# Output stores on another DMA queue, transposes one step earlier, and an exp ahead of an evacuation, in an attention + feed-forward kernel

## The chip, the cores and the metric

The kernel runs on one core of one Trainium2 chip. The metric is the device time of one execution in microseconds (us). Eight runs of the kernel before lie between 308.92 and 311.36 us, with a median of 310.46 us. A core has five engines with instruction queues of their own[...]: TensorE (PE: matrix multiplication into PSUM), VectorE (DVE), ScalarE (ACT), GpSimd (POOL) and SyncE (SP). In this kernel two of the queues issue DMAs: SP, whose transfers appear in the profile as the hardware queue q1, and POOL, whose transfers appear as the software queue q0. Both use the same 16 DMA engines.

## The reference

Attention for 8 batches of 8 heads, 576 tokens and head width 64. In front of each batch's keys and values stand 16 "beacon" keys and values that every query may see. The result is laid out as 4608 rows of 512 and goes through a feed-forward part:

```python
k_all = concatenate([beacon_k, k]);  v_all = concatenate([beacon_v, v])
a = softmax(q @ k_all.T / 8, causal on the 576 keys, free on the 16 beacons)
x = (a @ v_all) as 4608 x 512
h = (x @ w1) * (x @ w2) @ w3
out = h @ w_out            # 4608 x 512, float32
```

The last two products are linear, so the kernel forms `Wt = w3 @ w_out` once and then needs only `out = ((x @ w1) * (x @ w2)) @ Wt`. Matrix operands are fp16, sums and output are fp32.

## The kernel before

**Attention.** The work of a batch is cut into 8 steps `s`: four pairs of heads, two halves each (`NSB` = 8 steps a batch, `r = s % 8` is the place in the batch, `b = s // 8` the batch). A step needs `scores(s)` (line 446, two groups j = 0 and 1 of 4 to 10 matmuls, each into one of the two PSUM buffers `ps`), `exps(s, j)` (line 461, ACT: exp of `ps` into the SBUF tile `pT`), `mask(s, j)` (line 473, DVE: causal mask on the diagonal blocks; group 1 has none) and `values(s)` (6 or 24 matmuls with `va` on line 489, in even and odd steps, then the division by the row sums on DVE, lines 506 and 507, into `x16`).

**Feed-forward.** It is a Python generator, `stream()`, with one matmul of 512 columns to a unit. The 4608 rows are 9 chunks `mc` of 512. A chunk is 64 units of line 366 (`ff_ab`: for each of 8 column blocks a chain of four matmuls with w1, which ACT evacuates to `a_sb` on line 378, and a chain of four with w2, which DVE multiplies by `a_sb` into `gT` on line 380), and 32 units of line 400 (`ff_out`: four chains of eight matmuls with `Wt`; DVE evacuates each to `ot` on line 410, and line 411 stores the 128 x 512 fp32 tile, 256 KB, in HBM). `ot` has 8 buffers. All accumulations share three PSUM buffers `pm`. The evacuation is emitted with the last matmul of its chain.

**Order of the work.** The schedule is manual: each engine executes its instructions in the order in which the Python code emits them. The first 16 steps (batches 0 and 1) and the preparation of the weights follow the written list `ORDER`. Then 48 units are emitted, step 16's scores and exps, 8 more units and step 16's masks; and then the loop over steps 16 to 63 (lines 668 to 691), which mixes a number of units, `fill[s]`, into each step: 8 in steps 16 to 26, 12 or 13 in later ones. What is left when the steps are done (212 units) runs alone. One pass of the loop emits the scores and the first exp of step s + 1, `values(s)`, the first k1 of the units, the second exp and first mask of s + 1, and then the rest of the units. At 8 units a step, a step holds one whole column block: a chain with w1 and a chain with w2.

**Data of the batches.** `va`, `q16`, `k16`, `qT` and `kT` have two buffers, used by batches in turn. POOL issues the loads (lines 127, 136 and 140), which cast fp32 to fp16 on the way. At the end of the first pass of batch b (r = 0) it gets the `va` loads of batch b + 1, which must wait until step 8b - 1 has used the buffer, and behind them those of q and k of batch b + 2. SP issues the DMA transposes: `transpose_qk` (lines 151 and 152) makes `qT` and `kT` of batch b + 1 out of `q16` and `k16`, one of five chunks of tokens a pass, in passes r = 1 to 5; line 518 turns a finished batch's `x16` into columns of `xT` (two transposes in pass r = 6, three in pass r = 7), which the feed-forward part reads. SP also issues the stores of line 411. Each queue issues in the order in which the code emits, and each DMA queue has 8 semaphores in turn, so that a DMA also waits for the eighth one before it on its queue to land.

Of the kernel before, what the change touches and what calls it, by code (L numbers as in the profile page):

```python
# [12 lines left out]
ds, ts = bass.ds, bass.ts  # L13
# [50 lines left out]
def kernel(  # L64
# [13 lines left out]
    nc = tc.nc  # L78
    B, H, S, D = q.shape
    Nb = beacon_k.shape[2]  # L80
    P = 128
# [3 lines left out]
    M = B * S  # L85
    NKT = DM // P
    NFT = DF // P
    NJT = 5
# [36 lines left out]
    def load_q(b, c):  # L125
        rows = min(P, S - c * P)
        nc.gpsimd.dma_start(  # L127
            q16s[b % NB2][:rows, c, :].rearrange("s (h d) -> s h d", h=H),
            q[b, :, ds(c * P, rows), :].rearrange("h s d -> s h d"),
        )  # L130
# [11 lines left out]
    def load_k(b, jt):  # L142
        load_kv(b, jt, k, beacon_k, k16s[b % NB2][:, jt, :].rearrange("s (h d) -> s h d", h=H))

    def load_v(b, jt):
        load_kv(b, jt, v, beacon_v, vas[b % NB2][:, jt, :, 0:64])

    def transpose_qk(b, c):
        i = b % NB2
        rows = min(P, S - c * P)  # L150
        nc.sync.dma_start_transpose(qTs[i][:, :, ds(c * P, rows)], q16s[i][:rows, c, :])  # L151
        nc.sync.dma_start_transpose(kTs[i][:, :, ds(c * P, P)], k16s[i][:, c, :])  # L152
# [135 lines left out]
    for what, st in zip(FIRSTS[:7], homes):  # L288
# [7 lines left out]
        fill=0.0,  # L296
# [3 lines left out]
    for m, base in (  # L300
# [10 lines left out]
            fill=0.0,  # L311
# [84 lines left out]
    def ff_out(mc, gT):  # L396
        for mt in range(4):
            pm = psM.tile([P, 512], FP32, name="pm")
            for kf in range(NFT):
                nc.tensor.matmul(  # L400
                    pm,
                    gT[:, kf, ts(mt, P)],
                    Wt[:, kf, :],
                    start=(kf == 0),
                    stop=(kf == NFT - 1),
                )
                if kf < NFT - 1:
                    yield
            ot = op.tile([P, DM], FP32, name="ot")
            nc.vector.tensor_scalar(ot, pm, float(1.0 / GS), None, ALU.mult)  # L410
            nc.sync.dma_start(out[ds(mc * 512 + mt * P, P), :], ot)
            yield

    def stream():

        gT = yield from ff_ab(0, range(len(made), NFT), g0)
        yield from ff_out(0, gT)
        for mc in range(1, M // 512):
            gT = yield from ff_ab(mc)
            yield from ff_out(mc, gT)  # L420
# [6 lines left out]
    def emit_ff(n):  # L427
        nonlocal emitted
        for _ in range(n):
            try:  # L430
                next(ff)
            except StopIteration:
                return
            emitted += 1
# [17 lines left out]
    def scores(s):  # L452
        for j in range(2):
            score(s, j)

    def exps(s, j):
        g = 2 * (s % 2) + j
        if s // 2 not in pTs:
            pTs[s // 2] = ptp.tile([P, 2, PW], FP16, name="pT")
        pT = pTs[s // 2]  # L460
        nc.scalar.activation(  # L461
            pT[:, :, ds(GO[g], GW[g])], pss[s, j][:, :, 0 : GW[g]], AF.Exp, scale=scale
        )

    def mask(s, j):
        g = 2 * (s % 2) + j
        pT = pTs[s // 2]
        if g == 1:
            return
        m = {0: MA, 2: MB, 3: MB[:, 0:80]}[g]  # L470
        n = m.shape[1]
        blk = pT[:, :, ds(GO[g], n)]
        nc.vector.tensor_tensor(  # L473
            blk, blk, m.unsqueeze(1).to_broadcast([P, 2, n]), ALU.mult
        )
# [46 lines left out]
    def values(s):  # L522
        value_sums(s)
        normalize(s)

    NSB = 2 * NT
    NS = B * NSB
    fill = [0] * NS
# [7 lines left out]
    def ahead(s):  # L536
        scores(s)
        for j in range(2):
            exps(s, j)

    def masks(s):
        for j in range(2):
            mask(s, j)
# [119 lines left out]
        emit(*word.split("."))  # L663
    emit_ff(48)
    ahead(2 * NSB)
    emit_ff(8)
    masks(2 * NSB)
    for s in range(2 * NSB, NS):
        b, r = s // NSB, s % NSB
        more = s + 1 < NS  # L670
        if more:
            scores(s + 1)
            exps(s + 1, 0)
        values(s)
        k1 = min(4, fill[s])
        emit_ff(k1)
        if more:
            exps(s + 1, 1)
            mask(s + 1, 0)
        emit_ff(fill[s] - k1)  # L680
        if more:
            mask(s + 1, 1)
        if b < B - 1:
            if r == 0:
                for c in range(NJT):
                    load_v(b + 1, c)
                for c in range(NJT if b + 2 < B else 0):
                    load_q(b + 2, c)
                    load_k(b + 2, c)
            if 1 <= r <= NJT:  # L690
                transpose_qk(b + 1, r - 1)
    emit_ff(1 << 30)
# [1 line left out]
_INS = ['q', 'k', 'v', 'beacon_k', 'beacon_v', 'moe_w1', 'moe_w2', 'moe_w3', 'moe_w_out']  # L694
# [26 lines left out]
```

## Time and profile before

| what | value |
|---|---|
| median of 8 runs | 310.46 us |
| the profiled execution's own time | 310.35 us |
| its span, first to last instruction | 308.5 us |
| PE busy | 291.5 us (94% of the span) |
| DVE, ACT and POOL busy | 167.8, 157.9 and 114.6 us |
| granted PE clock, mean | 0.994 |
| DMA queues q0 and q1, share of 16 engines' span | 84.5% and 39.9% |
| HBM read and written | 39.32 and 9.44 MB |

The profile has one execution. Of a group of instructions it gives the busy time, the mean of one in ns, and the idle time of the engine ahead of them with what ended it. A timeline row gives start, duration, engine, line, operation, shape, the count, and in brackets the idle time before the first with what ended it; neighbours of one form are merged, so a row can be longer than the work in it. A matmul's end is modelled, so intervals from start to start are the safer measure.

### The profile page before, as it was taken

What the parts mean: (1) busy time and instruction counts of PE and PEld (TensorE: products, weight loads), DVE (VectorE), ACT (ScalarE), POOL (GpSimd) and SP (SyncE); (2) the same over time, 40 slices, a digit from 0 to 9 for tenths busy, and PEclk for the clock granted to TensorE, in tenths of its full rate; (3) what the DMA queues carried; (4) which work ended last, traced back from release to release, by engine and by line L of the source; (5) the groups of instructions that cost most, each with busy time, mean ns of one, the idle gap of its engine ahead of it and who ended that gap; (6) DMA issues with size and microseconds to landing.
All of it is one profiled execution on the core that took longest, in us unless ns stands there. A gap on an engine that the chain in (4) does not pass through costs nothing.

```text
span 308.5 us, 6956 instructions
## 1 busy us (share of the span) xinstructions
PE 291.5 (94%) x2804; PEld 148.4 (48%) x2804; DVE 167.8 (54%) x388; ACT 157.9 (51%) x224; POOL 114.6 (37%) x155
## 2 busy tenths in 40 slices
PE   7789989999889999979999999999999999999995
PEld 2345556554344455435555555455555554444442
DVE  5566757873455565535555555556555554343442
ACT  2448949921565666634566466546654660330320
POOL 4489498755645595049304930410000000000000
PEclk9999999999999999979999999999999999999999
DMA  7999999999999999999996999996333003302003
GB/s 277 307 159 183 186 151 168 141 138 145 230 141 155 156 142 212 149 162 162 170 199 77 160 195 156 114 193 125 72 75 141 0 12 70 135 0 102 34 2 136
DMA packets 162048, 42.67 MB, mean 138 GB/s; under 512 B 152288, under 2 KB 155872, under 8 KB 162016
## 3 DMA queue, kind: packets, MB, share of 16 engines
q0 software_dynamic: 109792, 17.57, 84.5%
q1 hardware_dynamic: 52224, 24.66, 39.9%
q8 instruction: 22, 0.36, 0.5%
q14 instruction: 10, 0.08, 0.1%
HBM read 39.32 MB, written 9.44 MB: 158 GB/s over the span
## 4 chain that ended last, share of the span: by engine, by line
PE 70%; DMA 13%; ACT 6%; POOL 3%; SPq 3%; DVE 2%; issue 2%; DVEq 0%; ACTq 0%
PE pm L366 32%; PE pm L400 18%; PE pv L489 9%; PE ps L446 7%; DMA qT<-q 5%; ACT pT L461 4%; DMA k<-in_k_dram 3%; DMA pT<-in_moe_w_dram 3%; PE pm L356 2%; DMA xT<-in_moe_w_dram 2%; ACT a_sb L378 2%; SPq L152 1%; POOL va L136 1%; DVE gT L380 1%; SPq L151 1%
## 5 line engine op out<-in xcount | busy, mean ns | idle before, releaser
L366 PE MATMUL pm<-xT,w 128*128 128x512 f16 x576 | 134.3, 382 | 0.5 <-ACT xT L232 0.5
L461 ACT ACTIVATE pT<-ps 128x768 f16<-128x768 f32 (+3 forms) x128 | 104.7, 864 | 41.9 <-PE ps L446 40.4
L366 PEld LDWEIGHTS <-w 128*128 128x128 f16 x576 | 53.6, 98 | 59.8 <-issue 3.3
L378 ACT ACTIVATE a_sb<-pm 128x512 f32<-128x512 f32 x69 | 41.2, 597 | 78.9 <-PE pm L366 78.3
L380 DVE TENSOR_TENSOR gT<-pm,a_sb 128x512 f16<-128x512 f32 x72 | 49.8, 691 | 49.8 <-PE pm L366 47.6
L400 PE MATMUL pm<-Wt,gT 128*128 128x512 f16 x288 | 65.8, 379 | 0.0
L136 POOL DMA_DIRECT2D va<-in_v_dram x40 | 33.8, 857 | 53.0 <-PE pv L489 46.8
L446 PE MATMUL ps<-qT,kT 64*128 64x80 f16 (+3 forms) x704 | 37.7, 228 | 5.3 <-ACT pT L461 2.9
L489 PE MATMUL pv<-va,pT 128*128 128x65 f16 x960 | 41.2, 194 | 1.5 <-DVE pT L473 1.5
L400 PEld LDWEIGHTS <-gT 128*128 128x128 f16 x288 | 27.2, 98 | 30.6
L489 PEld LDWEIGHTS <-pT 128*128 128x128 f16 x960 | 33.4, 98 | 12.0 <-issue 5.1
L506 DVE RECIPROCAL rd<-pv 128x4 f32<-128x4 f32 x64 | 12.1, 189 | 47.6 <-PE pv L489 47.2
L446 PEld LDWEIGHTS <-kT 64*128 64x128 f16 x704 | 20.7, 95 | 33.9 <-issue 32.4
L410 DVE TENSOR_SCALAR ot<-pm 128x512 f32<-128x512 f32 x36 | 24.9, 690 | 22.0 <-PE pm L400 21.9
L127 POOL DMA_DIRECT2D q<-in_q_dram x35 | 30.2, 863 | 12.1 <-DMA w<-in_moe_w_dram 3.7
L136 POOL DMA_DIRECT2D k<-in_k_dram x35 | 29.9, 855 | 9.5 <-DMA q<-in_q_dram 3.2
L507 DVE TENSOR_TENSOR x<-pv,rd 128x256 f16<-128x256 f32 x64 | 31.4, 491 | 2.4
L473 DVE TENSOR_TENSOR pT<-pT,MB 128x512 f16<-128x512 f16 (+1 forms) x64 | 20.7, 325 | 3.2 <-ACT pT L461 3.1
L473 DVE TENSOR_TENSOR pT<-pT,MA 128x480 f16<-128x480 f16 x32 | 12.8, 399 | 0.1
L356 PE MATMUL pm<-wo,wT 128*128 128x512 f16 x32 | 8.6, 381 | 0.2 <-DVE wT L351 0.2
L356 PE MATMUL ps<-wo,wT 128*128 128x512 f16 x32 | 7.9, 380 | 0.2
L340 PE MATMUL pm<-ident,xT 128*128 128x128 f16 x64 | 4.9, 220 | 3.3 <-DVE xT L568 2.2
(68 smaller groups left out, 100.2 us busy)
## 6 DMA issues: line engine op xcount, KB each, us to landing
out_dram<-ot SPq DMA_DIRECT2D x36, 256.0 KB, 4.0
q<-in_q_dram POOLq DMA_DIRECT2D x28, 128.0 KB, 8.9
va<-in_v_dram POOLq DMA_DIRECT2D x24, 128.0 KB, 6.6
k<-in_k_dram POOLq DMA_DIRECT2D x21, 128.0 KB, 8.9
w<-in_moe_w_dram POOLq DMA_DIRECT2D x4, 512.0 KB, 8.8
gT<-in_moe_w_dram SPq DMA_DIRECT2D x3, 512.0 KB, 6.3
gT<-in_moe_w_out_dram SPq DMA_DIRECT2D x2, 512.0 KB, 6.5
pT<-in_moe_w_out_dram SPq DMA_DIRECT2D x2, 512.0 KB, 9.1
```

Source lines behind the costliest of these rows:

```text
L127: nc.gpsimd.dma_start(q16s[b % NB2][:rows, c, :].rearrange("s (h d) -> s h d", h=H), q[b, :, ds(c * P, rows), :].rearrange("h s d -> s h d"),)
L136: nc.gpsimd.dma_start(dst[ds(p0, rows)], src[b, :, ds(s0, rows), :].rearrange("h s d -> s h d"))
L366: nc.tensor.matmul(pm, w12[:, kt, ds(i * DF + kf * P, P)], xT[:, kt, ds(mc * 512, 512)], start=(kt == 0), stop=(kt == NKT - 1),)
L378: nc.scalar.activation(a_sb, pm, AF.Copy, scale=GS)
L380: nc.vector.tensor_tensor(gT[:, kf, :], pm, a_sb, ALU.mult)
L400: nc.tensor.matmul(pm, gT[:, kf, ts(mt, P)], Wt[:, kf, :], start=(kf == 0), stop=(kf == NFT - 1),)
L410: nc.vector.tensor_scalar(ot, pm, float(1.0 / GS), None, ALU.mult)
L446: nc.tensor.matmul(ps[:, hh, ds(col, n)], kT[ds(hh * 64, 64), t, ts(jt, P)], qT[ds(hh * 64, 64), t, ds(q0, n)],)
L461: nc.scalar.activation(pT[:, :, ds(GO[g], GW[g])], pss[s, j][:, :, 0 : GW[g]], AF.Exp, scale=scale)
L473: nc.vector.tensor_tensor(blk, blk, m.unsqueeze(1).to_broadcast([P, 2, n]), ALU.mult)
L489: nc.tensor.matmul(pv[:, 2 * n + hh, 0:65], pT[:, hh, ds(col, P)], va[:, jt, 2 * t + hh, 0:65], start=(jn == 0), stop=(jn == len(BLK[i]) - 1),
L507: nc.vector.tensor_tensor(x16[:, ds(tiles[0], ni), ds(t * P, P)].rearrange("p i (h d) -> p i h d", h=2), pv[:, 0 : 2 * ni, 0:64].rearrange ...
```

## The change

1. In `ff_out` the stores of chunks 0 to 6 are issued by POOL (`nc.gpsimd`) and those of chunks 7 and 8 by SP as before. That is 28 of 36 stores.
2. The masks of step 16 are emitted ahead of the 8 units in front of the loop, not behind them.
3. In steps with fewer than 10 units, k1 is 3 and not 4. The fourth unit, which carries the evacuation of the chain with w1, is thereby emitted after the second exp of the next step.
4. `transpose_qk(b + 1, r)` runs in passes r = 0 to 4, not 1 to 5.

```diff
             nc.vector.tensor_scalar(ot, pm, float(1.0 / GS), None, ALU.mult)
-            nc.sync.dma_start(out[ds(mc * 512 + mt * P, P), :], ot)
+            queue = nc.gpsimd if mc < M // 512 - 2 else nc.sync
+            queue.dma_start(out[ds(mc * 512 + mt * P, P), :], ot)
             yield
...
     ahead(2 * NSB)
+    masks(2 * NSB)
     emit_ff(8)
-    masks(2 * NSB)
     for s in range(2 * NSB, NS):
...
         values(s)
-        k1 = min(4, fill[s])
+        k1 = 3 if fill[s] < 10 else 4
         emit_ff(k1)
...
-            if 1 <= r <= NJT:
-                transpose_qk(b + 1, r - 1)
+            if r < NJT:
+                transpose_qk(b + 1, r)
```

The order of instructions on PE is the same in both kernels. ACT's and DVE's change in the short steps alone. On SP no store stands among the transposes any more: the five of line 518 are followed at once by the ten of lines 151 and 152. On POOL the stores come in front of the load groups: 4 before that of pass 16, then 2, 3, 4 and 5 before those of passes 24, 32, 40 and 48, and 10 behind the last.

## The prediction

> **What bounds the kernel now.** First the busy rows of the page. PE is nearly full, so time can come back only where PE stands still or runs slowly.
>
> ```profile
> PE   7789989999889999979999999999999999999995
> PEclk9999999999999999979999999999999999999999
> DMA  7999999999999999999996999996333003302003
> ```
>
> A slice is 7.7 us. PE has 8s in slices 10 and 11 (77 to 93 us), stays a little under full to slice 13, and drops to 7 in slice 17 (131 to 139 us), where the granted clock drops too. From slice 22 on there is hardly a gap. The DMA engines show 9 until slice 20: transfers are a second resource to watch. So I read PE's timeline at those two places.
>
> ```profile
> 89.52 1.89 PE L366 MATMUL pm<-xT,w 128*128 128x512 f16 x8
> ...
> 91.97 0.40 PE L446 MATMUL ps<-qT,kT 64*128 64x256 f16 x4 [0.28 <-ACT pT L461]
> ...
> 95.66 0.35 PE L446 MATMUL ps<-qT,kT 64*128 64x80 f16 x10 [0.47 <-ACT pT L461]
> 95.95 0.36 PE L489 MATMUL pv<-va,pT 128*128 128x65 f16 x6
> 96.14 1.89 PE L366 MATMUL pm<-xT,w 128*128 128x512 f16 x8
> ...
> 106.27 1.89 PE L400 MATMUL pm<-Wt,gT 128*128 128x512 f16 x8
> ...
> 111.87 1.89 PE L400 MATMUL pm<-Wt,gT 128*128 128x512 f16 x8
> ```
>
> Two short steps with line 366 take 96.14 - 89.52 = 6.62 us. Two with line 400, same matmul counts, take 111.87 - 106.27 = 5.60 us. The difference is who evacuates: the chain of waits here runs through ACT.
>
> ```profile
> 89.69 0.88 PE pm L366 x4
> ...
> 90.59 0.60 ACT a_sb L378
> 91.19 0.74 ACT pT L461
> ...
> 91.97 0.40 PE ps L446 x4
> 92.36 0.84 PE pv L489 x24
> ```
>
> ACT waits for the w1 chain, evacuates it, only then runs the second exp, and PE's next scores need that exp's PSUM buffer. That is a loop through PE and ACT.
>
> ```profile
> 131.16 0.33 PE L446 MATMUL ps<-qT,kT 64*128 64x128 f16 x4
> 133.38 0.39 PE L446 MATMUL ps<-qT,kT 64*128 64x256 f16 x4 [1.89 <-DMA qT<-q]
> ...
> 134.55 4.32 PE L366 MATMUL pm<-xT,w 128*128 128x512 f16 x12
> ```
>
> This is the first use of batch 4's transposed q. PE waits 1.89 us for it, and the next 12 matmuls then take 4.1 us, where the same 12 elsewhere take 2.59. SP's own rows say why the transposes are late:
>
> ```profile
> 103.63 7.69 SPq L518 DMA_TRANSPOSE xT<-x  x5
> 111.41 3.44 SPq L411 DMA_DIRECT2D out_dram<-ot  x3
> 114.97 1.35 SPq L151 DMA_TRANSPOSE qT<-q  x1
> ```
>
> After the xT transposes SP stands until the third store's `ot` exists, and batch 4's first transpose starts at 114.97. The fourth q chunk, needed by the waiting scores, is issued at 125.02 and lands 8.22 later in the chain.
>
> **The exp ahead of the evacuation.** ACT's work in two steps is 785 + 1022 + 811 + 837 ns of exps and 2 x 597 of `a_sb`: 4.65 us, under PE's 5.60, so ACT fits once it no longer waits in the middle. From step 16's w1 chain (82.90) to step 23's chain (106.27) are 23.37 us. At line 400's pace the seven steps take three pairs of 5.60 and one of 3.14 (111.87 - 108.73): 19.94. At most 3.43 comes back. What is late next: `a_sb` starts when both exps are done, so `gT` waits for `a_sb`, and the mask of the next step's second group is behind `gT` on DVE, and the last 10 `values` matmuls of an odd step are behind that mask. Counting from the start of an even step's scores, with the rows' durations: exps end at 2.0, `a_sb` at 2.6, the w2 chain at 2.5, `gT` (0.69) at 3.35, the mask (0.23) at 3.5; those matmuls could start at 3.3. So 0.1 to 0.3 in each of four odd steps, of which line 400's pace already has 0.1. I take 0.5 in all, bounds 0 and 1.2: **2.9 us** back (2.2 to 3.4). Steps 24 to 26 hold only line 400: nothing there.
>
> **Step 16's masks.** In DVE's order the mask stands behind `gT`, which stood 1.80 us for `a_sb`; the wait list has 0.8 us of PE for it. Placed first, it needs only the exp that ended at 80.2, long before `values(16)`: **0.8 us** back.
>
> **Transposes and stores on SP.** PE now reaches step 23 3.7 us earlier, and SP's five xT transposes end near 111.3 - 3.7 = 107.6. No store follows, so batch 4's transposes start there and not at 114.97. Seven precede or are the fourth q chunk; at the spacing that they had (125.02 - 114.97 for six and a store) it is issued by 117.5 and with 8.2 lands by 125.7. PE needs it at 131.5 - 3.7 = 127.8. Earlier starts by the pass number alone cost nothing on PE: the buffers `qT` and `kT` are free since step 8b - 1's scores. Batch 4's q and k must have landed: the fourth chunk was issued by 102 and lands in a median of 7.5 to 8.4 in that stretch, about 110. So the wait goes: 1.89. Batch 6's 0.33 us wait (195.36) goes too.
>
> Whether the slow matmuls go with it is a choice.
>
> ```profile
> 131.50:133.40 1.90, 0.02 (x2) 0.05 (x4) 0.24 (x2) 0.78 (x1) 0.00 (x0) 1.00 1.61 157
> 134.50:136.00 1.50, 1.50 (x9) 0.62 (x7) 1.07 (x3) 0.37 (x1) 0.97 (x2) 0.50 1.69 176
> ```
>
> The window table's last columns are granted clock, DMA share and GB/s: directly behind the wait PE has half its clock, and full clock again from 138. [...] The trace's only dip within the work stands directly behind its longest wait after 20 us; waits of 0.82 and less have none (one of 1.53 at 8.8 us hasn't either, so it may hang on where a wait falls). The row decides: 4.13 - 2.59 = 1.54 on line 366 and 0.96 - 0.84 = 0.12 on the `values`, **3.55 us** with the wait, and 0.33 for batch 6. [...]
>
> **POOL's side.** 28 stores join 17.6 MB of loads. Issue: no store on POOL in the trace; nearest are line 258's 256 KB loads, 571 ns, and the 128-row loads of line 136, 857 ns for eight times the pieces. I take 0.6 us. Each waits for its `ot`, and the loads behind it wait too. Pass 16: four stores, all `ot` done by 79.9, before POOL is free at 80.93; `va` of batch 3 moves 2.4 us later, plus as much again if the eight semaphores pace them. Its last load was issued at 88.48 with 11.4 to land, so 99.9 becomes 102 to 105; `values(25)` needs it at 111.03 - 3.7 = 107.3. Pass 24: the second store's `ot` is ready near 111.4 - 3.7 = 107.7, against a `va` issue at 106.72: 1 to 2 us later, needed 25 us on. Passes 32, 40, 48: the last store in front is made within the pass's units, so the loads follow PE by some 5 us more than before, while PE is 7 earlier; `va` has 20 us of cover, q and k a batch. SP loses 28 issues of 0.33 to 0.56; nobody waited for those but the transposes. DMA bytes are the same. `ot` is reused 8 stores later, over 30 us: no wait. So 0; bounds -0.3 (transposes that land even earlier find no one waiting) and +2.
>
> [...]
>
> **Sum.** 310.35 (span 308.5 and 1.85 outside it) - 2.9 - 0.8 - 3.55 - 0.33 = 302.8. The median of the runs is 0.11 above the profiled one: **302.9 us**.
>
> **Rivals.** *A wait in place of the removed one.* Chunk 2's first matmuls (117.47) need the fourth xT transpose, issued near 108.5; at 5.9 us to landing it has 3 us of cover. With transposes close behind and more loads around it, 8.2 to 8.6 as for q is possible: 0.4 of cover. Or batch 4's q lands at 128 or later. Either costs 1 to 2 us and perhaps a clock dip of 1.7. For it: DMA at 9 in every slice there. Against: SP's stretch without stores. Time 304.5 to 306.5, 305.8 in the middle. *The exp gives nothing,* because `gT` and the mask take over the loop: 302.9 + 2.9 = 305.8; against it, 5.60 us pairs with the same DVE order. *Slower: loads behind stores.* Place: pass 16 on POOL. Batch 4's fourth chunks land near 110; they delay PE once they land after 127.8 - 8.2 - 1.3 = 118.3. It takes 8 us of delay to matter, and then 7.6 minus a 1.7 dip, about 6, to eat the gain: four stores that cost 14 us, 3.5 each, decide it. Beyond that, with the next groups equally late, 312 to 316.
>
> **How the numbers follow.** Likeliest case 0.60 (302.9; own range 301.9 to 304.2); replaced wait 0.22; no gain from the exp 0.08; slower by late loads 0.07; gains that just cancel 0.03. 0.3% is 0.9 us, about what a measurement of this kernel can tell. Faster: 0.60 + 0.21 + 0.07 = 0.88; same 0.04; slower 0.08. The range starts at the upper bounds (3.4 + 0.8 + 3.55 + 0.33 leaves 302.3) less 0.6 for spread, and reaches over most of the replaced wait and the lost exp: 301.7 to 306.6.
>
> **What would show it.** Right: pairs of short steps at 5.6 to 5.8 us; ACT with two exps in a row ahead of `a_sb`; no PE wait on `qT` near 128; granted clock full in every slice; SP's first transpose of batch 4 near 107.6; POOL's stores at 0.6 us. Wrong: pairs still over 6.2, with `values` waiting for the mask; a wait on `xT`, `va` or `qT` between 100 and 130; a clock dip with no wait ahead of it; POOL rows of 2 us and more.

## The result, and the profile after

| | before | after |
|---|---|---|
| median of the runs (n; lowest to highest) | 309.98 us (32; 308.29 to 312.19) | 306.63 us (11; 303.87 to 310.77) |
| profiled execution: own time; span | 310.35; 308.5 us | 303.87; 301.9 us |
| ratio of the runs, after to before | | 0.987, 95% interval 0.984 to 0.989 |

The change makes the kernel 1.3% faster, about 4.2 us (0.0134 x 309.98). The forecast had the direction, but its 302.9 us was too low by 3 to 4 us (the kernel takes 305.8 us by the ratio, 306.63 by the median). The profiled execution of after, 303.87 us, is the fastest of its eleven; seven of the others took 305 to 307 us and three 308.8 to 310.8. The ratio leaves out runs more than 1.5% above the fastest of their kernel, these last three among them, so it says a little more than the two medians, which are 3.35 us apart.

The busy rows of after's page. A slice is 7.5 us now:

```profile
PE   7889989999999999999999999999999989999994
PEclk9979999999999999999999999999999999999999
DMA  7999999999999999999999999999991014103003
```

The 8s of slices 10 and 11 and the 7 of slice 17 are gone from PE. The clock drops once, to 7 tenths in slice 2 (the first slice is 0; 15 to 23 us), where the weights are prepared: 3.41 us of half clock from 19.20. The DMA engines are as full as before, but for longer: 9 until slice 29, where before has 9 until slice 26, with one 6.

PE's timeline in the short steps of after:

```profile
88.24 1.89 PE L366 MATMUL pm<-xT,w 128*128 128x512 f16 x8
90.06 0.55 PE L447 MATMUL ps<-qT,kT 64*128 64x128 f16 x8
90.55 1.06 PE L490 MATMUL pv<-va,pT 128*128 128x65 f16 x24
91.45 1.89 PE L366 MATMUL pm<-xT,w 128*128 128x512 f16 x8
...
93.92 1.89 PE L366 MATMUL pm<-xT,w 128*128 128x512 f16 x8
```

A pair of steps is 93.92 - 88.24 = 5.68 us long, and no row here has a bracket: PE waits for nobody. The chain of waits there holds PE alone, where ACT's evacuation and exp stood in it before:

```profile
88.84 1.29 PE pm L366 x6
90.13 0.48 PE ps L447 x8
90.62 1.00 PE pv L490 x24
91.61 1.73 PE pm L366 x8
```

SP's timeline at the turn of the batch, and PE's where it needs batch 4's transposed q:

```profile
100.47 7.34 SPq L519 DMA_TRANSPOSE xT<-x  x5
107.92 1.50 SPq L151 DMA_TRANSPOSE qT<-q  x1
...
117.59 1.28 SPq L151 DMA_TRANSPOSE qT<-q  x1
```

```profile
127.70 0.55 PE L447 MATMUL ps<-qT,kT 64*128 64x128 f16 x8
128.19 0.90 PE L490 MATMUL pv<-va,pT 128*128 128x65 f16 x24
128.93 2.75 PE L366 MATMUL pm<-xT,w 128*128 128x512 f16 x12
```

The transposes start at 107.92 (forecast: near 107.6), the fourth q chunk is issued at 117.59 (117.5). It landed at 126.80 in the trace, 0.9 us before PE's scores at 127.70 (125.7 and 127.8 were forecast, a cover of 2.1). So the wait is gone, by less than half the cover that the forecast gave it. The window table shows full clock behind it (columns: span of the window, busy time of PE, its weight loads, DVE, ACT and POOL, then granted clock, DMA share, GB/s):

```profile
126.00:130.00 4.00, 4.00 (x46) 2.09 (x44) 2.42 (x7) 1.90 (x4) 2.10 (x3) 1.00 1.79 145
```

To see where the time went I cut the span of each profile at three matmuls: the first of line 400 in the whole kernel, the first of line 400 for chunk 1 (the end of the slow short steps), and the last scores of step 63. In us:

| profile | start | short steps | middle | end | span |
|---|---|---|---|---|---|
| before | 72.05 | 34.21 | 145.47 | 56.78 | 308.51 |
| after | 72.61 | 30.20 | 141.22 | 57.83 | 301.86 |
| difference | +0.56 | -4.01 | -4.25 | +1.05 | -6.65 |

The short steps and the middle gave 8.3 us. The end took 1.05 back, and the start, which the change does not touch, happened to be 0.56 longer.

POOL's part of the page's costliest groups, and of its landing times:

```profile
L412 POOL DMA_DIRECT2D out_dram<-ot x28 | 15.5, 557 | 60.3 <-DVE ot L410 42.5
```

```profile
out_dram<-ot POOLq DMA_DIRECT2D x28, 256.0 KB, 8.1
q<-in_q_dram POOLq DMA_DIRECT2D x28, 128.0 KB, 10.3
va<-in_v_dram POOLq DMA_DIRECT2D x24, 128.0 KB, 9.7
```

A store costs POOL 557 ns (forecast: 0.6 us). But transfers land later than in the profile of before: `va`'s loads 9.7 us after issue where they took 6.6, q's 10.3 where they took 8.9. That is one execution of each kernel: in the second profiles, below, `va`'s loads take 7.2 us in after and 7.5 in before, and q's 9.7 in both. And POOL stands 42.5 us for `ot`, with the loads of the next batches queued behind.

### The profile page after: what moved, and what is told of

Read it like the earlier page. It is cut to its first block, busy times and chain, and to the rows that moved or that the text cites. A ratio compares the mean times of both kernels' runs of the same rounds, so it can differ in the third digit from the quotient of the medians.

```text
span 301.9 us, 6967 instructions
## 1 busy us (share of the span) xinstructions
PE 290.4 (96%) x2804; PEld 149.2 (49%) x2804; DVE 167.1 (55%) x388; ACT 158.3 (52%) x224; POOL 130.4 (43%) x183
## 4 chain that ended last, share of the span: by engine, by line
PE 87%; DMA 5%; ACT 2%; POOL 2%; DVE 1%; issue 1%; SPq 1%; DVEq 0%; ACTq 0%
PE pm L366 41%; PE pm L400 21%; PE pv L490 12%; PE ps L447 10%; DMA xT<-in_k_dram 3%; PE pm L356 2%; DMA pT<-in_moe_w_dram 2%; ACT pT L462 1%; POOL q L170 0%; DVE gT L380 0%; POOL k L170 0%; SPq L274 0%; PE pm L227 0%; POOL xT L258 0%; PE pm L195 0%
## 5 line engine op out<-in xcount | busy, mean ns | idle before, releaser
L366 PE MATMUL pm<-xT,w 128*128 128x512 f16 x576 | 132.7, 379 | 0.5 <-ACT xT L232 0.5
L412 POOL DMA_DIRECT2D out_dram<-ot x28 | 15.5, 557 | 60.3 <-DVE ot L410 42.5
L447 PE MATMUL ps<-qT,kT 64*128 64x80 f16 (+3 forms) x704 | 36.1, 228 | 0.6 <-ACT pT L462 0.4
L356 PE MATMUL ps<-wo,wT 128*128 128x512 f16 x32 | 8.8, 411 | 0.2
## 6 DMA issues: line engine op xcount, KB each, us to landing
q<-in_q_dram POOLq DMA_DIRECT2D x28, 128.0 KB, 10.3
```

What stands on the lines that cost most here:

```text
L366: nc.tensor.matmul(pm, w12[:, kt, ds(i * DF + kf * P, P)], xT[:, kt, ds(mc * 512, 512)], start=(kt == 0), stop=(kt == NKT - 1),)
L447: nc.tensor.matmul(ps[:, hh, ds(col, n)], kT[ds(hh * 64, 64), t, ts(jt, P)], qT[ds(hh * 64, 64), t, ds(q0, n)],)
```

## The experiments

The question was what the median holds above the forecast, and which part of the change brings the gain. One answer: executions differ by their start alone, and each part gives what the traces of after show. The rival: the stores on POOL, in front of the loads, make transfers late in some executions, so that PE waits where the profiled execution of after does not. In the texts below that were written ahead of each run, theory L is this rival; rival D is that the 16 DMA engines are simply full; theory P, later, is that POOL's queue has no room for the stores.

The table gives each timed kernel's median and ratio to the kernel before, and the three cuts of its one profile (start, short steps, middle, end). The ratio is the comparison to trust; a profile is one execution.

| kernel | median us (n) | ratio (95%) | start, short, middle, end |
|---|---|---|---|
| after, again | 305.60 (6) | 0.984 (0.980 to 0.988) | 73.59, 30.20, 141.22, 57.83 |
| parts 2, 3, 4; stores on SP | 305.12 (6) | 0.985 (0.981 to 0.990) | 74.72, 30.20, 143.52, 56.79 |
| part 1 alone | 308.03 (20) | 0.993 (0.991 to 0.995) | 74.63, 34.21, 141.22, 57.83 |
| parts 2 and 3 alone | 309.40 (22) | 0.998 (0.995 to 1.000) | 73.03, 30.21, 148.65, 56.79 |
| loads ahead of the stores | 307.87 (6) | 0.983 (0.977 to 0.989) | 73.54, 30.19, 148.63, 57.83 |
| stores held, on SP | 303.25 (6) | 0.977 (0.973 to 0.981) | 75.21, 30.20, 141.90, 56.79 |
| stores held, again | 303.92 (6) | 0.979 (0.974 to 0.983) | 72.73, 30.20, 141.53, 56.79 |
| no stores of chunks 0 to 6 | 302.61 (6) | 0.977 (0.973 to 0.980) | 73.37, 30.21, 141.22, 57.49 |
| stores twice, on POOL | 330.93 (4) | none given | 71.94, 31.08, 167.62, 57.85 |
| stores held and twice, on SP | 309.69 (20) | 0.998 (0.996 to 1.001) | 72.63, 32.13, 147.23, 57.04 |

### The changed kernel again, twice, and the kernel before again

No edit: two more profiles of after, one with times, and one of before.

> The changed kernel once more, to get a second profiled execution and more times. In the first one (303.87 us) PE stands nowhere, but the median is 306.63. Theory L (load groups held behind stores on POOL): batch 7's q and k land late, its transposes are only 0.4 to 1.3 us ahead of scores(56) and scores(57) in the first profile, so other executions wait there. Median 306 to 307; if the profiled execution is over 305, it has a PE wait on qT or kT near 217 to 222 us, with or without half a clock window behind it. Rival D (the DMA engines are simply full): waits are scattered over the batches, on xT, va or qT.

> The changed kernel once more, for a third profiled execution. Short steps 30.2 and end 57.8 as before. If its time is over 305.5, the middle is over its floor of 141.2 by a PE wait on qT or kT of batch 7 (steps 55 to 57), as in the run with the loads first (5.5 us there), with half a clock window or two behind it; if the middle is at the floor, the rest is the start.

> The kernel before once more, for a second profiled execution. By phases: start to the first matmul of line 400 72 to 75 us, short steps 34.2, then to the last scores 141.2 (the floor without waits) plus the waits of SP's stores and transposes: 143 to 147, end 56.8. If the middle is at 141.2 and the start at 77, then the scatter and the median are the start's alone.

The short steps are 30.20 us in all three profiles of after, and 34.21 and 34.22 in the two of before: this part of the gain is the same every time. The start is not: 72.61, 73.59 and 73.44 against 72.05 and 74.02, with the same instructions. The middle is 141.22 twice, and 143.01 in the third profile, whose own time is 306.50, about the median of the first set of runs. PE's timeline there:

```profile
116.65 2.75 PE L366 MATMUL pm<-xT,w 128*128 128x512 f16 x12 [1.63 <-DMA xT<-x]
```

PE waits 1.63 us for chunk 2's first matmuls. SP's row shows no late issue:

```profile
101.30 7.25 SPq L519 DMA_TRANSPOSE xT<-x  x5
```

The fourth of these five was issued at 105.92 and landed at 116.51, 10.6 us later; the forecast gave it 5.9, and 8.2 to 8.6 in its rival. This is that rival, *a wait in place of the removed one*, at its place and inside its price of 1 to 2 us, without the clock dip that it allowed for. The expectations for these two runs looked elsewhere, at `qT` and `kT` of batch 7, where no profile of after has a wait; and the second set's median, 305.60, lies below the expected 306 to 307.

The second profile of before is of use for the other side of the sum:

```profile
135.74 0.39 PE L446 MATMUL ps<-qT,kT 64*128 64x256 f16 x4 [2.27 <-DMA qT<-q]
```

```profile
135.70:137.00 1.30, 1.26 (x29) 0.99 (x30) 0.00 (x0) 0.00 (x0) 0.00 (x0) 1.00 1.71 153
137.00:139.00 2.00, 2.00 (x11) 0.92 (x10) 1.70 (x4) 1.51 (x2) 1.73 (x3) 1.00 1.89 155
```

The wait is there, and longer than 1.89, but the clock behind it is 1.00. So the 1.66 us of slow matmuls, which I took from one row, are not lost in each execution of before, and the change cannot give them back in each.

What differs between the two traces is where the wait lies. Where a trace has several stretches of half clock, their starts lie whole multiples of 3.413 us apart: in before 134.32 and 308.40, or 51 slots of such a grid; in after 19.20 and, behind the last instruction, 302.51, or 83; between the two of the kernel with stores held and twice 71.68 us, or 21; between the four in the steps of the kernel with stores twice on POOL 20, 11 and 4. Divided at its trace's grid, the wait of before falls into one slot, and that of the second profile into two. First before, then the second profile; the second number is PE's busy time in the slot:

```profile
130.91:134.32 3.41, 1.52 (x30) 0.88 (x29) 0.83 (x2) 0.78 (x1) 0.00 (x0) 1.00 1.72 156
134.32:137.73 3.41, 3.41 (x18) 1.39 (x15) 1.40 (x4) 1.51 (x2) 2.70 (x4) 0.50 1.70 169
```

```profile
130.73:134.14 3.41, 2.74 (x16) 1.03 (x14) 2.21 (x5) 2.01 (x4) 0.13 (x1) 1.00 1.81 155
134.14:137.55 3.41, 1.81 (x32) 1.28 (x33) 0.51 (x2) 0.26 (x2) 0.28 (x1) 1.00 1.79 155
137.55:140.97 3.42, 3.42 (x34) 1.61 (x33) 1.77 (x5) 3.09 (x5) 3.42 (x5) 1.00 2.04 168
```

In before PE is idle for 1.89 us of a slot, and the next slot has half clock. In the second profile it is idle for 0.67 and 1.60 us of two slots, and no slot has. Between 60 us and the last scores, in all fourteen traces, half clock followed each of the nine full-clock slots with 1.89 us or more of idle PE, and none with 1.60 or less.

### Stores on SP, with the other three parts

```diff
-            queue = nc.gpsimd if mc < M // 512 - 2 else nc.sync
-            queue.dma_start(out[ds(mc * 512 + mt * P, P), :], ot)
+            nc.sync.dma_start(out[ds(mc * 512 + mt * P, P), :], ot)
```

> The changed kernel with all stores back on SP: parts 2, 3 and 4 without part 1. Theory L: POOL's load groups are early again, so nothing is late in batch 7; batch 4's first transpose stands behind two stores, near 108, as early as in the changed kernel. 302.9 to 304, with a narrower scatter than the changed kernel's 303.9 to 310.8. Rival D: the same DMA work in the same time, so 306 to 307 again.

0.985 here and 0.984 with the stores on POOL, on one chip: moving the stores to the other queue is worth nothing that can be measured once the transposes begin a step earlier (each interval is 0.4% wide to either side, so 1 us could hide in them). The median, 305.12, is neither theory's. The profile's middle has three short waits on transfers (0.59, 0.84 and 0.35 us) where after's first two have none, and its end is 1.04 us shorter. The trace names ACT for the wait of 0.84, which ended at 131.76; the q chunk for these scores had landed at 131.62.

### Part 1 alone, and parts 2 and 3 alone

The kernel before with the edit of part 1:

```diff
-            nc.sync.dma_start(out[ds(mc * 512 + mt * P, P), :], ot)
+            queue = nc.gpsimd if mc < M // 512 - 2 else nc.sync
+            queue.dma_start(out[ds(mc * 512 + mt * P, P), :], ot)
```

> The kernel before with part 1 alone. My prediction's terms: SP's xT transposes end at 111.3, batch 4's transposes start there and not at 115, and the 1.89 us wait and the slow clock window behind it go: 310.0 - 3.5 = 306.5. Theory L: the load groups are late against PE here too, but PE is 3.7 us later than in the changed kernel, so part of the gain stays: 306.5 to 308.5, with waits on qT in the last batches. Rival that part 1 gives nothing: 310.

The kernel before with the edits of parts 2 and 3:

```diff
+    masks(2 * NSB)
     emit_ff(8)
-    masks(2 * NSB)
...
-        k1 = min(4, fill[s])
+        k1 = 3 if fill[s] < 10 else 4
```

> The kernel before with parts 2 and 3 alone (masks of step 16 first, second exp ahead of the evacuation). The sum says 3.7 us less at step 23: pairs of short steps at 5.6 to 5.8 us. The stores on SP come earlier with PE, so batch 4's wait on qT stays about 1.9 us and the clock window with it: 306 to 306.6. If the earlier PE uncovers the transposes further (rival D), the wait at scores(32) grows to 3 to 5 us: 308 to 310.

Part 1 alone leaves the short steps at 34.21 and takes the wait on `qT` away (middle 141.22): ratio 0.993. That is 308.03 us where the forecast's terms gave 306.5; of the missing 1.5 us, 1.05 are in the end, which is longer. Parts 2 and 3 alone make the short steps 30.21, as in after, and win next to nothing: 0.998. Their profile says where the 4 us went:

```profile
115.03 2.75 PE L366 MATMUL pm<-xT,w 128*128 128x512 f16 x12 [0.42 <-DMA xT<-x]
132.00 0.40 PE L446 MATMUL ps<-qT,kT 64*128 64x256 f16 x4 [2.96 <-DMA qT<-q]
...
168.31 0.35 PE L446 MATMUL ps<-qT,kT 64*128 64x80 f16 x10 [0.70 <-DMA kT<-k]
```

The third row is from a later stretch of the same timeline. PE arrives 4 us earlier, the transposes do not, and so the wait on `qT` grows from 1.89 to 2.96 us, with a half-clock window behind it, and waits on `xT` and `kT` appear. The sum in the forecast added the two gains as if each stood alone. Alone they give 0.7% (part 1) and 0.2% (parts 2 and 3), all together 1.3 to 1.6%: the faster short steps need an earlier transpose to be worth anything. Part 4 does that as well as part 1: parts 2 and 3 alone give 0.998, and with part 4 0.985. Where the stores are on POOL, though, part 4 changes no order: in passes 0 to 4 as in passes 1 to 5, SP gets the same transposes one behind the other, since nothing stands between those of `xT` and those of the next batch. No run shows this; it follows from the code.

### Loads ahead of the stores

```diff
         values(s)
+        if b < B - 1 and r == 0:
+            for c in range(NJT):
+                load_v(b + 1, c)
+            for c in range(NJT if b + 2 < B else 0):
+                load_q(b + 2, c)
+                load_k(b + 2, c)
```

(and the same group is taken out of the end of the pass.)

> The changed kernel, with each batch's load group emitted at the start of pass r = 0, ahead of that pass's units, and so ahead of the store that is made within the pass. Reference point: part 1 alone has a median of 308.0 with no wait between the short steps and the last scores; less the 4.0 that the short steps give, an execution of the changed kernel without waits should take about 304.0. Theory L (load groups held behind POOL's stores make batch 7 late): the group no longer waits for the pass's own store, some 4 us earlier; median 304 to 304.8 and the scatter of part 1 alone (3.3 us). Rival D (DMA engines full; PE is early against all transfers of batches 3 and 4): 305.5 to 306.6, scatter 6 us or more, as the changed kernel.

This did not settle anything. The median is above what either theory gave. The runs lie between 303.20 and 312.24 us, the ratio's interval covers those of after, and the profile caught the worst of them:

```profile
222.22 0.34 PE L447 MATMUL ps<-qT,kT 64*128 64x128 f16 x4
228.07 0.51 PE L447 MATMUL ps<-qT,kT 64*128 64x80 f16 x10 [5.51 <-DMA kT<-k]
```

SP issued the last of that batch's transposes at 215.03; it landed at 228.03, 13.0 us later, and the scores waited until 228.07, with 6.8 us of half clock around. The order of loads and stores on POOL alone does not take the scatter away.

### Stores held back on SP, and no stores

In the first five passes of a batch, the pass's stores are put into a list, and issued on SP behind the pass-4 transposes; otherwise the kernel is after.

```diff
-            queue = nc.gpsimd if mc < M // 512 - 2 else nc.sync
-            queue.dma_start(out[ds(mc * 512 + mt * P, P), :], ot)
+            held_out.append((mc * 512 + mt * P, ot))
+            if not holding[0]:
+                flush()
...
+        holding[0] = b < B - 1 and r < NJT
...
                 transpose_qk(b + 1, r)
+            if r == NJT - 1:
+                flush()
```

> The changed kernel with all stores on SP, but those made in passes r = 0 to 4 held back until the batch's ten transposes are issued (at most 4 of the 8 ot buffers wait). Load groups are never behind a store, transposes never behind one. Theory L: 303 (the 304.0 floor less the 1.0 that POOL kernels have at the end), scatter 3 to 4 us. Rival D: 304.5 to 305.5, waits on qT, kT or xT near 117 to 136 as with the stores on SP (0.59, 0.84 and 0.35 there).

> The kernel with the stores held back on SP once more, for more executions and a second profile. Theory P (POOL's queue is short of places for the stores): 302.5 to 304 in the median, all runs under 307, short steps at 30.2 us, the middle within 1 us of its floor of 141.2. If the first result was luck of few runs, 304.5 to 306.5 as the changed kernel.

The next kernel bounds what any placing of these stores can give:

```diff
-            queue = nc.gpsimd if mc < M // 512 - 2 else nc.sync
-            queue.dma_start(out[ds(mc * 512 + mt * P, P), :], ot)
+            if mc >= M // 512 - 2:
+                nc.sync.dma_start(out[ds(mc * 512 + mt * P, P), :], ot)
```

> The changed kernel without the stores of chunks 0 to 6 (28 of 36 are left out, so its output lacks them): 7.3 MB less for the DMA engines, POOL and SP free of them. Both theories: the floor, 303 (304.0 less 1.0), scatter of 3 to 4 us. If it stays at 305 or more with a scatter of 6, neither the stores' place nor their load is the cause, and it lies ahead of them, in the start up to 72 us or in the loads themselves.

Without the 28 stores the ratio is 0.977. With all of them, held on SP, it is 0.977 and 0.979 in two sets; the highest run of twelve is 306.12 us. After has 0.984 and 0.987, so with the stores on POOL it is slower by 0.5 to 0.9% of 310 us, about 2 to 3 us. (The first set of after lies clear of all three; the second, 0.980 to 0.988, overlaps a little with the second of the held version, 0.974 to 0.983.) The forecast had 0 for that, and its 302.9 us is close to what the kernel takes without the 28 stores, 302.61. The held version thus saves all that can be told of what the stores cost, and it beats both kernels. The later time seems to do it, not the queue: on SP without holding them the ratio was 0.985. Its SP timeline at the turn of the batch:

```profile
103.07 7.30 SPq L527 DMA_TRANSPOSE xT<-x  x5
110.48 0.53 SPq L421 DMA_DIRECT2D out_dram<-ot  x1
111.11 1.45 SPq L151 DMA_TRANSPOSE qT<-q  x1
```

One store that was already made goes in front and costs SP 0.6 us; the chunk's other three are held back, so SP no longer stands for their `ot`. In before it stood 3.44 us there.

The landing times do not explain it. These are those of the second profile of the held version:

```profile
out_dram<-ot SPq DMA_DIRECT2D x36, 256.0 KB, 5.9
q<-in_q_dram POOLq DMA_DIRECT2D x28, 128.0 KB, 11.3
va<-in_v_dram POOLq DMA_DIRECT2D x24, 128.0 KB, 11.6
```

Loads land later here than in after, and the kernel is faster. `xT`'s transposes land after a median of 4.9 and 5.9 us in the two profiles of before, 7.2, 6.0 and 7.1 in the three of after, 7.8 and 7.6 in those of the held version, 7.3 with the stores on SP and 7.1 with parts 2 and 3 alone; without the 28 stores they take 5.1, and with part 1 alone 3.7. So landing tends to be slower when the short steps are faster and the stores are there, on whichever queue they are; but the two kernels nearly meet (5.9 and 6.0), so single profiles do not prove it.

Of the 2 to 3 us, 1.05 can be placed in the traces: the end is 57.83 or 57.84 us in every profile with single stores on POOL and 56.78 to 56.80 in every one with single stores on SP. Without the 28 stores it is 57.49. That splits it. About 0.7 us is in the closing of the program, which takes 1.74 us from the last store's landing in after and 1.04 in before: after the last store SP checks semaphores one by one, in both traces in the same order. In after, with only 8 stores and the transposes on SP, the last store's is in the third of nine checks, and six more and a drain take 0.85 us behind it (300.17 to 301.02); in before it was in the seventh, and two more and the drain took 0.16 (307.52 to 307.68). That is the same without the 28 stores (57.49 against 56.78 for the end), so it goes with how many DMAs SP has issued, not with POOL. The other 0.35 us is in step 63, in PE's timeline of after:

```profile
248.55 0.46 PE L490 MATMUL pv<-va,pT 128*128 128x65 f16 x10 [1.02 <-DVE pT L474]
```

That wait is 0.67 us in before and in the held version: a `gT` starts 0.4 us later on DVE there and holds up the mask. I have not found why.

### Every store twice

Each of the 28 stores is followed by a second one, of the same tile, into a spare tensor in HBM; once on POOL in after, once on SP in the held version.

```diff
             queue.dma_start(out[ds(mc * 512 + mt * P, P), :], ot)
+            if mc < M // 512 - 2:
+                queue.dma_start(spare[ds(mc * 512 + mt * P, P), :], ot)
```

> The changed kernel with each of POOL's 28 stores followed by a second one of the same tile to spare rows of HBM: the suspected cost doubled. Theory L: waits appear in the last batches first, PE on qT or kT at scores(56) and scores(57), some 5 to 8 us; 309 to 315. Rival D: waits appear already at steps 24 to 33, on xT, va or qT. If the time stays within 1 us of the changed kernel's, the stores on POOL cost nothing and the scatter has another cause.

> The kernel with the stores held back on SP (303.25 us), with each of the first 28 stores followed by a second one of the same tile to spare rows of HBM: the same extra bytes as in the run with doubled stores on POOL (330.9 us, PE waits of 1 to 4.5 us in every batch from step 24 on). Theory P (POOL's queue is what is short[...]): on SP the same bytes cost little, 303.5 to 306, and at most small waits. Rival D (the DMA engines' capacity is what is short): the extra bytes cost the same wherever they are issued, 320 to 331.

The same 7.3 MB more (28 x 256 KB) cost 24.3 us on POOL (330.93 - 306.63; 18 with the lowest of its four runs, 324.91) and 6.4 us on SP (309.69 - 303.25). Both are more than theory L and theory P gave, and the second is far below rival D's 320 to 331. Both kernels move the same bytes, so the capacity of the DMA engines alone does not make the difference; place and queue, which differ together here, do. The waits of PE on transfers in the kernel with two stores on POOL (columns: us in total, times, longest):

```profile
PE ps L451 <- DMA qT<-q: 11.5, 3, 4.5
PE pv L494 <- DMA va<-in_v_dram: 3.6, 1, 3.6
PE ps L451 <- DMA kT<-k: 2.1, 2, 1.1
```

At and behind these waits PE had half clock for 20.5 us in all. POOL itself waits in that kernel:

```profile
POOL spare_rows L414 <- DMA k<-in_k_dram: 20.0, 11, 5.2
```

In after's trace none of 162 DMAs on POOL was issued before the eighth one ahead of it on its queue had landed, and 64 were issued within 0.5 us of that landing; in before's none of 134 was issued earlier. On SP the eighth one ahead had landed 3.2 us or more before each of the 126 issues of before and the 98 of after, so SP did not stand for one. With the 8.1 to 10.3 us to landing of after's page, eight in flight make one issue each 1.0 to 1.3 us, by this estimate. In before, POOL had room: it stood 46.8 us for `values` ahead of the `va` loads, in four waits. In after that wait is not among its largest; the stores' wait for `ot` and the queue have taken its place:

```profile
POOL out_dram L412 <- DVE ot L410: 42.5, 7, 22.1
POOL k L136 <- DMA va<-in_v_dram: 12.4, 9, 2.0
POOL va L136 <- DMA k<-in_k_dram: 7.3, 6, 2.2
POOL q L127 <- DMA va<-in_v_dram: 7.1, 5, 2.1
```

## Why the prediction was right in sign and too low in size

**The exp ahead of the evacuation and step 16's masks: right.** Forecast 2.9 and 0.8, together 3.7 us; measured 4.01, in each profile with parts 2 and 3 and each store once, to 0.02. Pairs of steps are 5.68 us (forecast 5.6 to 5.8), and no `values` waits for a mask in the short steps; of the 0.5 us that I had kept for later masks, 0.2 was lost (3.43 + 0.8 - 4.01). The rival *the exp gives nothing* is out. What the step did not say is that it has no value alone: by itself it won 0.24%.

**The wait on `qT`: right as to the wait, mis-sized as to the clock.** With each store issued once, it is gone from the middle wherever part 1 or part 4 is in, except for the 0.84 us in the profile with stores on SP. For the slow matmuls I took the row of before as it stood, as if half clock followed each such wait. It did follow waits of 1.89 us (before), 2.96 (parts 2 and 3 alone) and 1.91 and 2.12 (held and twice), each time for 3.4 us. But none followed 2.27 us in the second profile of before, nor 1.63 in the third of after. The slots of 3.413 us tell these apart: half clock followed where 1.89 us or more of idle PE fell into one slot, and not where 1.60 or less did. In the two profiles of before the wait lay differently against the slots, and the one trace that I had did not show that. So the 1.66 us (1.54 + 0.12) was a term to weigh with a chance, and I took it whole.

**POOL's stores at 0: the step that failed.** The working had the issue time right (557 ns for 0.6 us) and found cover for each late load, one by one, with the landing times of before. Two things were wrong with that. First, landing times were held fixed while PE became faster. They are not: the median for `xT`'s transposes was 4.9 us in the trace that I used and 6.0 to 7.2 in those of after, the fourth took 10.6 in one profile, where I had 5.9, and its 3 us of cover were used up; `qT`'s cover was 0.9 where I had 2.1. This tends to come with the faster steps, on whichever queue the stores are. Secondly, against the held version and the one without them the stores on POOL cost 2 to 3 us, which is the size of the miss. Of these 1.05 us is the end of the kernel, which the forecast did not cost at all, and 0.7 of that is no matter of POOL; the other 1 to 2 us I can't place: the wait of 1.63 us in one profile would be of that size. My upper bound, +2, was near; the value taken was not. Doubled, the stores cost 24 us, so POOL's queue was close to where PE pays for more transfers.

**Transposes a step earlier at 0: right here, for a reason that I had not given.** With part 1 in place it changes no order on SP, POOL or PE. Without part 1 it is the part that matters.

**From the profile to the median.** I made the sum against one execution and added 0.11. The start of the kernel, which nothing here touches, took 71.9 to 75.2 us in the fourteen profiles, and that of before was, at 72.05, the second shortest; at the same time that execution had a clock dip which the other profile of before lacks. In the median of before the two may cancel; once the change removes the dip, they do not. The result lies where the rival *a wait in place of the removed one* put it (304.5 to 306.5; here 305.8 by the ratio, 306.63 by the median), and one of three profiles of after shows its wait, on `xT` at 116.65, one of the signs of being wrong. The likeliest case, with its own range of 301.9 to 304.2, did not come. That the wider range, 301.7 to 306.6, holds the result is due to its having been stretched over that rival, and the median stands at its very edge.

**Slower by late loads: not seen.** Batch 4's q and k were late by nothing that PE met, and the four stores of pass 16 took POOL 2.2 us, not 14.

What stays open: whether the runs of after without a profile hold waits like the one on `xT` (three profiles, one with it), which would be the 1 to 2 us (half clock is not what makes the longest ones: 310.63 and 310.77 us had the same mean clock, 0.994, as the fastest); why landing times differ so between executions of one kernel; and the 0.35 us in step 63.

## What to carry to other kernels

Before adding a gain in one stage to a gain in the next, ask whether the second stage's supply moves with the first: here 4 us of faster steps were worth 0.24% until the transposes moved too. A queue that seems to have slack because it waits for a buffer need not be free for new work (POOL stood 46.8 us for `values` in before, and the 28 stores on it cost 2 to 3 us against the held version): price added transfers by what queues behind them, and take cover with the landing times of a busier execution, not with those of one profile of before. If stores must leave a queue's critical stretch, try first to issue them later on the same queue; it beat a move to the other one, 0.977 to 0.979 against 0.984 to 0.987.

## What the runs showed of the hardware

- Half clock came in slots of 3.413 us, at whole multiples of that within a trace (51 slots apart in before, 83 in after). Between 60 us and the last scores of the fourteen traces it followed each of the nine full-clock slots in which PE was idle for 1.89 us or more, and none with 1.60 or less; so the wait of 1.89 us in before had it, and the one of 2.27 in before's second profile, 0.67 and 1.60 in two slots, had not. The wait of 5.51 us with the loads first had two slots of half clock, 6.8 us.
- A 256 KB store took POOL 540 to 591 ns to issue in after, and SP a median of 0.33 us in before, at most 0.56. On POOL it landed a median of 8.1 us later in after; the 8 stores left on SP, which run when the loads are over, landed in 2.0.
- Doubling 28 stores cost 24.3 us on POOL's queue, which also carries the loads, and 6.4 on SP's, which has the transposes, held back behind them, at equal bytes.
- The last store's check was the third of SP's nine at the end of the program in after and the seventh in before; from its landing to the end of the span it took 1.74 us and 1.04, with nothing changed in the last stores themselves.
